# FFT-style convolution on one core: pixel loads of the next tile issued with the jobs that free their buffers, scratch loads and inverse jobs later, last planes sooner

## The chip, the cores and the metric

One core of a Trainium2 chip. The metric is device microseconds of one execution, the median over several runs. One execution of each kernel was also taken by the hardware profiler; the times within it are microseconds from the start of its span. Engines are called as the profile calls them: PE (TensorE matmuls), PEld (its weight loads), DVE (VectorE), ACT (ScalarE), POOL (GpSimd), SP (SyncE, which here only issues DMAs).

## The reference

A circular convolution of a 224x224 image of 96 channels with a 7x7 kernel, written through FFTs:

```python
wp = jnp.pad(w, ((0, H - K), (0, W - K), (0, 0), (0, 0)))
Xf = rfft2(x.astype(float32), axes=(1, 2))
Wf = rfft2(wp.astype(float32), axes=(0, 1))
Yf = jnp.einsum('bhwi,hwio->bhwo', Xf, Wf)
y = irfft2(Yf, s=(H, W), axes=(1, 2)).astype(bfloat16)     # x: 1x224x224x96, w: 7x7x96x96, bf16
```

## The kernel before

The kernel cuts the image into seven tiles of 32 columns. In each tile it transforms along the height with small matmuls (the forward jobs: pixels `xn` to spectra `xf`), convolves along the width for each of 17 spectral slots (the rounds, 33 matmuls each, on `xf` and on sums and differences `J` of it, the planes), writes the result to a scratch in DRAM (`scr`), loads it back in another layout (`tt`) and transforms back (the inverse jobs). Rounds of a tile are the frame; jobs of neighbouring tiles are slipped into each half round, so that PE stays full. DVE combines a round's products in two steps (`u` and `v`) and POOL adds them (the sum, `yf`), now and then DVE; POOL also copies the few columns that a tile shares with the tile before (the halo). Tiles 0 and 1 are convolved together in rounds r = 0 to 20, tile 1 four rounds behind; tile 2's forward jobs are part of that. Then tiles 2 to 6 follow one after another.

Each engine executes in program order, and SP issues nearly all DMAs: its order is the order in which the program text calls them. The four pixel buffers are reused by every tile.

```python
def pace(q, k):                 # q = [first half round, last, jobs, how many]
    a, b, jobs, n = q
    if k < a: return
    due = n if k >= b - 1 else -(-n * (k - a + 1) // (b - a))
    while jobs and n - len(jobs) < due:
        jobs.pop(0)()

def pump():                     # scratch loads, at most NTT = 5 tt buffers held
    while pend and held[0] < NTT:
        load_t(*pend.pop(0)); held[0] += 1
...
bursts = {}                     # (round, tile) -> which tile's planes are made there by DVE
for g in range(len(JGB)):       # groups of three slots, the last of two
    ...
    r1 = LAG + g0 - 1
    bursts[(r1, 0 if r1 < NS else 1)] = (1, g)
bursts[(NS + LAG - 1, 1)] = (2, 0)          # NS = 17, LAG = 4
for r in range(NS + LAG):
    for p in range(3):          # tile 2's forward jobs, in three parts
        if r == SH2[p + 1] + 1 - (p == 2):
            new_xf(2, SH2[p], SH2[p + 1])
            fj = f_jobs(2, p)   # p == 2: four jobs, two for each pair of pixel buffers
            if p == 2:
                fj += [lambda c=c: load_x(c) for c in range(12, 16)]     # tile 3's pixels
            add(2 * r, 2 * r + (8, 7, 4)[p], fj)
    if r == NS + 1:
        queue_c(0)              # tile 0's first scratch loads
    ...                         # the rounds of tiles 0 and 1
for t in range(2, NT):
    add(0, 26, a_jobs(t + 1))   # forward jobs of the next tile; starts with POOL's halo copy
    k1 = 2 * NS if t < TL else 2 * NS - 6
    km = 3 + -(-(k1 - 3) * nold // (nold + nnew))
    add(3, km, cj[:nold])       # inverse jobs
    ...
```

## Time and profile before

| | before |
|---|---|
| time, median (range) | 303.24 us (301.99 to 303.66, 4 runs) |
| PE busy, of a span of 300.3 us | 273.1 us, 91% |
| longest wait of PE in the program's middle | 8.16 us, for xn |
| half clock after it | 109.8 to 120.05 us |

A line of a timeline gives start, length, engine, operation, result and operands, their shape and how many instructions were merged; in brackets stands how long the engine had been idle and what ended that.

### The profile page before, as it was taken

The numbers are of one execution on the slowest core, as the hardware profiler recorded it, in microseconds if no ns is written. First come the engines' busy times: TensorE is split into PE (matmuls) and PEld (weight loads), VectorE is DVE, ScalarE is ACT, GpSimd is POOL, SyncE is SP. The second block draws the span as 40 slices with busy tenths as digits, with TensorE's granted clock in tenths as the row PEclk, the third lists the DMA queues.
The fourth block names the chain that finished last, engine by engine and source line by source line (L and its number), as shares of the span: only waits on it lengthen the run. The fifth ranks groups of instructions, "written<-read, shape, count | busy, mean of one in ns | idle before, by whom it ended". The sixth has DMA issues, their size and how long they took to land.

```text
span 300.3 us, 11988 instructions
## 1 busy us (share of the span) xinstructions
PE 273.1 (91%) x5010; PEld 246.0 (82%) x5010; DVE 227.9 (76%) x472; ACT 196.3 (65%) x488; POOL 112.3 (37%) x151
## 2 busy tenths in 40 slices
PE   8598998999999736999989999899999999999993
PEld 3488998989999726989889989798888989788872
DVE  7857399889797643686988879877897889967823
ACT  2456984766863412888578876788779875676313
POOL 6814022546536650234183235324264223243100
PEclk9955999999999985999999999999999999999998
DMA  7993340112111397577748686687727743776965
GB/s 179 170 219 98 83 123 35 41 43 81 44 41 43 106 201 219 143 188 197 219 105 224 195 224 195 187 218 211 232 89 185 224 138 102 197 197 174 251 127 183
DMA packets 45830, 46.04 MB, mean 153 GB/s; under 512 B 33626, under 2 KB 34758, under 8 KB 45678
## 3 DMA queue, kind: packets, MB, share of 16 engines
q1 hardware_dynamic: 43488, 43.21, 53.6%
q10 hardware_dynamic: 2288, 2.06, 2.4%
q8 instruction: 39, 0.64, 0.9%
q14 instruction: 15, 0.12, 0.1%
HBM read 23.92 MB, written 21.33 MB: 151 GB/s over the span
## 4 chain that ended last, share of the span: by engine, by line
PE 59%; DMA 13%; DVE 12%; issue 4%; ACT 4%; SPq 4%; POOL 1%; DVEq 0%; ACTq 0%; POOLq 0%
PE pb L86 59%; DVE J L86 5%; SPq L86 4%; DMA wq<-in_w_dram 3%; DVE v L86 2%; DMA xn<-in_x_dram 2%; DVE WF L86 2%; DMA xf<-scra 2%; ACT xf L86 2%; DVE u L86 2%; DMA scra<-yf 2%; DMA xf<-scrb 1%; DVE yf L86 1%; DMA scr<-yf 1%; ACT WF L86 1%
## 5 line engine op out<-in xcount | busy, mean ns | idle before, releaser
L86 PE MATMUL pb<-WF,J 96*128 96x96 bf16 x2898 | 169.9, 208 | 3.3 <-DVE J L86 2.2
L86 PEld LDWEIGHTS <-J 96*128 96x128 bf16 (+1 forms) x2910 | 144.2, 98 | 18.5 <-issue 9.9
L86 POOL TENSOR_TENSOR yf<-v,u 128x384 bf16<-128x384 f32 x85 | 83.9, 999 | 155.3 <-issue 103.6
L86 ACT CAST xf<-pb 96x408 bf16<-96x408 f32 (+3 forms) x150 | 68.3, 482 | 21.3 <-PE pb L86 18.8
L86 ACT CAST yo<-pb 84x384 bf16<-84x384 f32 (+1 forms) x144 | 61.3, 480 | 6.0 <-PE pb L86 4.5
L86 DVE TENSOR_TENSOR J<-xf 96x1824 bf16<-96x1824 bf16 (+1 forms) x84 | 63.2, 792 | 0.0
L86 PE MATMUL pb<-WF,xf 96*128 96x96 bf16 x952 | 61.0, 208 | 2.1 <-DVE WF L86 2.0
L86 PE MATMUL pb<-Fm,xn 118*128 118x136 bf16 (+3 forms) x576 | 52.4, 218 | 11.0 <-DMA xn<-in_x_dram 8.2
L86 PEld LDWEIGHTS <-xf 96*128 96x128 bf16 x952 | 47.8, 98 | 2.6 <-issue 1.5
L86 PEld LDWEIGHTS <-xn 118*128 118x128 bf16 x576 | 34.5, 101 | 12.5 <-DMA xn<-in_x_dram 8.3
L86 PE MATMUL pb<-tt,Gm 102*84 102x384 bf16 (+1 forms) x144 | 35.8, 329 | 0.6 <-DVE J L86 0.4
L86 ACT CAST WF<-pb 96x480 bf16<-96x480 f32 (+1 forms) x62 | 30.7, 570 | 5.1 <-PE pb L86 4.8
L86 PE MATMUL pb<-wq 98*128 98x120 bf16 (+1 forms) x336 | 26.3, 233 | 2.4 <-DMA wq<-in_w_dram 2.4
L86 DVE TENSOR_TENSOR J<-J 96x912 bf16<-96x912 bf16 (+1 forms) x42 | 27.6, 658 | 0.0
L86 PEld LDWEIGHTS <-wq 98*128 98x128 bf16 (+1 forms) x336 | 23.6, 151 | 3.9 <-POOL ct L86 2.6
L86 DVE TENSOR_TENSOR yf<-v,u 128x384 bf16<-128x384 f32 x27 | 15.4, 570 | 0.9
L86 POOL COPY xf<-xf 96x816 bf16<-96x816 bf16 (+3 forms) x16 | 15.7, 1010 | 0.0
L86 PEld LDWEIGHTS <-Gm 102*84 102x84 bf16 (+1 forms) x144 | 11.5, 114 | 3.0 <-DMA tt<-scr 0.6
L86 PE MATMUL pb<-wu 128*112 128x384 bf16 (+1 forms) x60 | 12.8, 376 | 1.1 <-DVE ct L86 1.1
L86 PEld LDWEIGHTS <-wu 128*112 128x112 bf16 (+1 forms) x60 | 7.3, 123 | 5.9 <-issue 1.9
L86 DVE TENSOR_TENSOR WF<-WF 96x960 bf16<-96x960 bf16 x15 | 11.1, 787 | 0.1
L86 DVE CAST xf<-pb 96x408 bf16<-96x408 f32 (+1 forms) x18 | 8.6, 516 | 1.9 <-PE pb L86 1.9
(388 smaller groups left out, 205.1 us busy)
## 6 DMA issues: line engine op xcount, KB each, us to landing
xn<-in_x_dram SPq DMA_DIRECT2D x28, 336.0 KB
scr<-yf SPq DMA_DIRECT2D x30, 288.0 KB
tt<-scr SPq DMA_DIRECT2D x24, 288.0 KB
out_dram<-yo SPq DMA_DIRECT2D x24, 252.0 KB
tt<-scr SPq DMA_DIRECT2D x12, 192.0 KB
out_dram<-yo SPq DMA_DIRECT2D x12, 168.0 KB
out_dram<-tt SPq DMA_DIRECT2D x4, 336.0 KB
scr<-yf SPq DMA_DIRECT2D x6, 192.0 KB
```

What stands on the lines that cost most here:

```text
L86: r = fn(*a, **k)
```

## The change

Its intent is to remove the hole in PE between the common stage of tiles 0 and 1 and tile 2. The whole of it is order:

```diff
-        r1 = LAG + g0 - 1
+        r1 = LAG + g0 - (3 if g == len(JGB) - 1 else 1)
         bursts[(r1, 0 if r1 < NS else 1)] = (1, g)
-    bursts[(NS + LAG - 1, 1)] = (2, 0)
+    bursts[(NS + LAG - 2, 1)] = (2, 0)
...
                 if p == 2:
-                    fj += [lambda c=c: load_x(c) for c in range(12, 16)]
-                add(2 * r, 2 * r + (8, 7, 4)[p], fj)
+                    for i in (1, 3):
+                        def fin(f=fj[i], i=i):
+                            f()
+                            for h in range(2):
+                                load_x(12 + 2 * h + i // 2)
+                        fj[i] = fin
+                add(2 * r, 2 * r + (8, 7, 5)[p], fj)
...
-        if r == NS + 1:
+        if r == NS + 3:
             queue_c(0)
...
-        km = 3 + -(-(k1 - 3) * nold // (nold + nnew))
-        add(3, km, cj[:nold])
+        k0 = 10 if t == 2 else 3
+        km = k0 + -(-(k1 - k0) * nold // (nold + nnew))
+        add(k0, km, cj[:nold])
```

## The prediction

> **What bounds the kernel now.** I read the page first, for the engine that is busiest and the place where it is not.
>
> ```profile
> span 300.3 us, 11988 instructions
> PE 273.1 (91%) x5010; PEld 246.0 (82%) x5010; DVE 227.9 (76%) x472; ACT 196.3 (65%) x488; POOL 112.3 (37%) x151
> ...
> PE   8598998999999736999989999899999999999993
> ...
> PEclk9955999999999985999999999999999999999998
> ```
>
> PE (the matmuls) is busy 91% of the span, so the time is PE's work plus PE's holes. In the slices of 7.5 us there is one hole away from the two ends: the digits 7, 3, 6 (98 to 120 us), and the granted clock falls to 8 and 5 in the last two. The program there ends the stage in which tiles 0 and 1 are convolved together and starts tile 2, which is exactly where the change works. Next I asked for the busy time in stretches cut at that hole (columns: PE, PEld, DVE, ACT, POOL busy, clock, DMA share, GB/s).
>
> ```profile
> 102.00:107.40 5.40, 3.55 (x80) 3.26 (x76) 3.33 (x9) 0.96 (x3) 1.83 (x2) 1.00 0.73 146
> 107.40:115.50 8.10, 0.00 (x0) 0.01 (x1) 2.30 (x4) 0.32 (x1) 2.77 (x4) 0.65 1.13 214
> 115.50:120.00 4.50, 4.48 (x53) 4.50 (x54) 2.72 (x5) 1.78 (x4) 0.00 (x0) 0.50 0.56 205
> 120.00:145.00 25.00, 25.00 (x497) 23.19 (x496) 18.38 (x40) 20.39 (x53) 7.89 (x8) 1.00 0.65 179
> ```
>
> For 8.1 us no matmul runs while DMA is full; then PE is busy again but at half clock until 120; from 120 PE has no idle time at all, and DVE (74%) and ACT (82%) have room. So a microsecond taken from this hole should shorten the kernel by one. The timeline of PE names what ends each hole:
>
> ```profile
> 104.04 0.34 PE L86 MATMUL pb<-WF,J 96*128 96x96 bf16 x4 [1.80 <-DVE J L86]
> ...
> 106.85 0.50 PE L86 MATMUL pb<-WF,xf 96*128 96x96 bf16 x8
> 115.52 0.50 PE L86 MATMUL pb<-Fm,xn 118*128 118x136 bf16 x3 [8.16 <-DMA xn<-in_x_dram]
> 115.81 1.33 PE L86 MATMUL pb<-WF,J 96*128 96x96 bf16 x14
> ...
> 119.13 1.20 PE L86 MATMUL pb<-WF,J 96*128 96x96 bf16 x14
> ```
>
> Two holes: 1.80 us for the last planes J of tile 1, and 8.16 us for the first pixels (xn) of tile 3, whose forward transform is interleaved with tile 2. Groups of 14 matmuls take 1.33 and 1.20 us after it; the same group takes 0.76 us from 121.6 us on. Why the pixels come so late is told by SP's queue, which issues all these loads in program order, and by the chain of work:
>
> ```profile
> 102.75 6.25 SPq L86 DMA_DIRECT2D tt<-scr  x10
> 109.11 5.38 SPq L86 DMA_DIRECT2D xn<-in_x_dram  x8
> 115.18 0.83 SPq L86 DMA_DIRECT2D scr<-yf  x2
> ```
>
> ```profile
> 99.39 3.31 DMA scr<-yf
> ...
> 106.92 2.09 SPq L86
> ...
> 109.49 5.89 DMA xn<-in_x_dram
> ```
>
> The pixels stand behind ten scratch loads (tt). Those cannot start before tile 0's last scratch write has landed (99.39 + 3.31 = 102.70), they then take until 109.0 to issue, and the pixel load takes 5.89 us behind their traffic. The buffers were free at about 100.8, when the last tile-2 forward matmuls ended. The path is thus: scratch write, tt issue, xn load, PE.
>
> **What the Trainium skill says.** "DMA: Bandwidth & Descriptors", section "Anatomy of one DMA", says that DMA engines do not wait on semaphores: any wait is on the issuing sequencer, before dispatch. The trace agrees: SP is silent from 99.71 to 102.75, and xn, which needed nothing from scratch, was held too. The same page, section "Specifications", puts the least transfer for line rate at 512 B. The tt packets here are 384 B: 226 GB/s at a DMA share of 1.02 (104 to 106 us), against 321 GB/s at 0.88 where mostly 3 KB pixel packets move (116 to 118), so it agrees in direction. "TensorE: Matmul & The Clock Gate", section "What's actually happening", says that an idle window of about 3.4 us halves the clock and a busy one restores it. Here the clock fell at 109.8, 2.5 us after the last matmul, and came back at 120.05, 4.5 us after the first: the windows are free-running, so only the size agrees. "GPSIMD Engine Reference", section "Specifications", says POOL shares its SBUF interfaces with VectorE. The trace agrees: the 96x912 plane sum takes 0.62 us alone (109.08) and 1.28 us while POOL copies the halo (153.90).
>
> **The change, part by part.** No arithmetic is added or removed: the built instruction streams have 10022 PE, 444 DVE, 67 POOL and 227 SP rows in both, and only two evacuations change to ACT (326 to 328 rows). Everything is order. (A round is one spectral slot's convolution, 33 matmuls; in each of its two halves waiting jobs of other stages are slipped in. xn 12 to 15 are tile 3's four pixel loads.)
>
> 1. Pixel loads. Each pair of tile 3's loads now follows the forward job that reads its two buffers last, and the tt loads are queued two rounds later. On SP the order becomes: last scratch write of tile 0, eight xn issues, the next scratch write, ten tt issues. I date this from the old trace. Forward job 1 ends on PE at about 99.8. SP must first pass tile 0's last write, which waits for POOL's sum. That sum was done at 99.37, but part 3 puts 1.39 us of planes (1.01 + 0.46, overlapped, at 102.97) in front of it: 100.75. Then xn 12 issues at about 101.2, xn 14 at 101.9, and 13 and 15 follow job 3 (PE, about 102.3). A pixel load with an idle DMA took 3.2 to 3.35 us from issue to its last semaphore step (the loads at 33 to 43 us), so xn 12 lands at 104.5 to 105, and the last of the four near 108.
> 2. When is xn 12 needed? PE reached that place at 107.35; without the J hole at 105.55. Margin 0.5 to 1 us, so the 8.16 us go. The second buffer (13) is needed six half rounds later, about 110: safe.
> 3. Planes. Tile 1's last planes move from round 18 to 16, ahead of use by three rounds: the 1.80 us go. Tile 2's first planes move one round up; in the old order they ran from 107.76 to 109.7 inside the xn hole, and would otherwise have become a new hole of over 1 us. In the new order their first operation ends near 105.2 and is needed near 105.6.
> 4. Clock. With no hole of several us, the half clock between 115.52 and 120.05 goes: half of 4.53 us, 2.27 us.
> 5. Inverse jobs of tile 2 start at half round 10 rather than 3: the same 12 jobs in 24 instead of 31 half rounds. This moves PE work, and it keeps PE from waiting for the tt loads, which now issue from about 104.8 and land by about 113; half round 10 is at 105.5 + 5 rounds of 1.75 us, about 114.
>
> Given back: about 0.3 us in round 18, because a PSUM bank waits for a DVE operation that now stands behind the moved planes (PE comes at 99.8, DVE frees it at 100.1); and about 1.1 us near tile 2's start. There DVE has a sum and three plane operations while POOL copies the halo, as at tile 3's start, where PE waited 1.09 us for DVE u (155.50) and at tile 4's about 1.0. In the old run this was masked: the halo copy ran at 110.7 inside the hole.
>
> Sum: 8.16 + 1.80 + 2.27 - 0.3 - 1.1 = 10.8 us. From the median of 303.2: 292.4 us.
>
> **Rivals.** (a) The pixels are still late. SP is one queue, and each issue also waits for the DMA eight before it; if the scratch write is released later, or the load is slowed by the 480 KB written just before it (those writes took 3.3 to 3.8 us against 2.07 alone), xn 12 lands 1 to 2 us late: 294 to 295. For: the margin is thin. Against: the DMA share is only 0.23 from 96 to 102.
> (b) DVE becomes the bound. Rounds 0 to 4 of tile 2 now lack inverse jobs: PE has 33 convolution matmuls (1.39 us) and two forward jobs (0.36), 1.75 us; DVE has about 1.7 us (u and v 0.81 at their spacing, a third of 2.0 us of planes and 0.57 of sum, about 0.86). Nearly equal, so 1 us more could be lost: 293.5.
> (c) The denser inverse jobs bind ACT or DMA. In rounds of two xf and two yo evacuations ACT is busy 82 to 84% and PE 100% (120 to 135 us), so ACT should hold. DMA was at 0.95 share from 130 to 135; my estimate for the new dense stretch is 220 GB/s, and five tt buffers give many us of slack. If it binds, 2 to 3 us: 295.
> (d) Nothing gained, because the hole moves to another wait. Against it: from 120 to 145 us PE is full, so no other chain is near.
>
> **Range and chances.** (a), (b) and (c) each cost 1 to 3 us and seldom all together; on the other side the 1.4 us given back may be absent: 290.5 to 296.0. Two per cent is 297.2, so faster needs only 6 of the 10.8 us: 0.95. Same 0.04, slower 0.01.
>
> **What would show it.** Right: no PE wait for xn, the J wait of 1.80 us gone, clock 1.00 from 31 us to the tail, xn issued near 101 before tt, a DVE wait of about 1 us within tile 2's first four rounds, none on tt. Wrong: a PE wait for xn of over 1 us near 105, a clock drop there, PE waits for tt after half round 10, or waits that make tile 2 much longer than 32 us from its first round to tile 3's (before: 106.85 to 149.33, less the 8.16 and 2.27).

## The result

The changed kernel takes 292.48 us (290.70 to 292.68, 4 runs) against 303.24: faster, ratio 0.9639 with a 95% interval of 0.9592 to 0.9686. It is the mean time of the one kernel's fast runs over that of the other's (292.08 over 303.03), so it is not quite the ratio of the two medians. In a second set of timing rounds (e9 below) it was 0.9647.

The page of the kernel after, the same four lines as before:

```profile
span 291.0 us, 11983 instructions
...
PE 272.5 (94%) x5010; PEld 244.2 (84%) x5010; DVE 229.6 (79%) x472; ACT 195.8 (67%) x488; POOL 113.1 (39%) x151
...
PE   8598998999999998999899998999999999999982
...
PEclk9955899999999999999999999999999999999997
```

PE's busy time is what it was (272.5 against 273.1 us); the digits 7, 3, 6 in its middle are gone and so is the dip of the clock. The stretches (PE, PEld, DVE, ACT, POOL busy, clock, DMA share, GB/s):

```profile
102.00:107.40 5.40, 5.40 (x131) 5.29 (x128) 4.30 (x10) 2.61 (x6) 3.12 (x5) 1.00 1.00 258
107.40:115.00 7.60, 6.55 (x141) 6.23 (x139) 7.13 (x12) 4.34 (x12) 5.77 (x6) 1.00 1.16 220
115.00:120.00 5.00, 4.73 (x97) 4.38 (x95) 4.53 (x11) 3.77 (x10) 1.96 (x2) 1.00 1.01 271
```

What was one empty stretch now holds 141 matmuls at full clock beside the same full DMA. About a microsecond of idle time is left in it, and DVE is busy 94% there (7.13 of 7.60). PE's timeline says where:

```profile
105.02 0.50 PE L86 MATMUL pb<-WF,xf 96*128 96x96 bf16 x8
105.41 0.34 PE L86 MATMUL pb<-Fm,xn 118*128 118x136 bf16 x3
...
110.55 0.34 PE L86 MATMUL pb<-WF,J 96*128 96x96 bf16 x4 [0.52 <-DVE J L86]
...
111.76 0.47 PE L86 MATMUL pb<-WF,J 96*128 96x96 bf16 x7 [0.53 <-DVE J L86]
```

The first matmuls on tile 3's pixels follow the last before them without a wait. Two holes of half a microsecond, for planes, are new. SP's queue shows the new order:

```profile
101.30 3.10 SPq L86 DMA_DIRECT2D xn<-in_x_dram  x8
105.07 0.34 SPq L86 DMA_DIRECT2D scr<-yf  x1
105.46 9.30 SPq L86 DMA_DIRECT2D tt<-scr  x10
```

And the chain of work no longer passes through a DMA or through SP in this stretch (start, length, what):

```profile
95.95 13.26 PE pb L86 x331
...
110.42 1.29 DVE J L86
...
111.76 4.02 PE pb L86 x85
```

Where did the time come from? The copy that ACT makes in the first round of a tile marks that tile's start: tile 2 at 107.44 before and 105.60 after (1.84 us sooner), tile 3 at 150.05 and 139.62 (10.43), tile 6 at 252.52 and 242.12 (10.40). So the gain is made before tile 3 and carried on unchanged (tile 0's start gives 0.12 us of it: 27.39 and 27.27). The two traced spans differ by only 9.3 us: the traced run of before was its fastest and that of after its slowest, and the traced tail differs (PE waits 1.13 us for a last scratch load, xf, in the run after). The medians differ by 10.8.

### The profile page after: what moved, and what is told of

Its sections match the earlier page's. It is cut to its first block, busy times and chain, and to the rows that moved or that the text cites. A ratio compares the mean times of both kernels' runs of the same rounds, so it can differ in the third digit from the quotient of the medians.

```text
span 291.0 us, 11983 instructions
## 1 busy us (share of the span) xinstructions
PE 272.5 (94%) x5010; PEld 244.2 (84%) x5010; DVE 229.6 (79%) x472; ACT 195.8 (67%) x488; POOL 113.1 (39%) x151
## 4 chain that ended last, share of the span: by engine, by line
PE 65%; DVE 14%; DMA 5%; issue 5%; POOL 4%; ACT 4%; SPq 1%; DVEq 0%; ACTq 0%; POOLq 0%
PE pb L86 65%; DVE J L86 6%; POOL ct L86 3%; DVE v L86 2%; DMA tt<-scr 2%; DVE u L86 2%; DMA xf<-scrb 2%; ACT xf L86 2%; DVE WF L86 1%; DVE yf L86 1%; DVE ct L86 1%; ACT WF L86 1%; POOL yf L86 1%; SPq L86 1%; DMA scrb<-yf 1%
## 5 line engine op out<-in xcount | busy, mean ns | idle before, releaser
L86 DVE TENSOR_TENSOR J<-xf 96x1824 bf16<-96x1824 bf16 (+1 forms) x84 | 64.4, 806 | 0.0
L86 DVE TENSOR_TENSOR J<-J 96x912 bf16<-96x912 bf16 (+1 forms) x42 | 28.3, 674 | 0.0
L86 POOL COPY xf<-xf 96x816 bf16<-96x816 bf16 (+3 forms) x16 | 16.7, 1073 | 0.0
L86 ACT CAST tt<-pb 112x384 bf16<-112x384 f32 x8 | 3.6, 479 | 9.7 <-PE pb L86 9.6
```

The costliest lines, as they stand in the source:

```text
L86: r = fn(*a, **k)
```

## The experiments

Ten runs, on the same chip in each group, each beside the kernel before. Times at the start (tile 0 began anywhere from 26.8 to 29.0 us) and at the tail vary by more than a microsecond from run to run, so besides the time I compare tile starts and PE's holes within the traces. A run that is over 1.5% above the fastest of its kernel counts as slow and is left out of the ratios; only e5 has such runs. A trace is one run, so differences of a few tenths between traces are less sure than the ratios.

### e1_loads_only: the pixel loads alone

The kernel before, with:

```diff
-                    fj += [lambda c=c: load_x(c) for c in range(12, 16)]
-                add(2 * r, 2 * r + (8, 7, 4)[p], fj)
+                    for i in (1, 3):
+                        def fin(f=fj[i], i=i): ...        # as in the change
+                        fj[i] = fin
+                add(2 * r, 2 * r + (8, 7, 5)[p], fj)
```

> Kernel before with the pixel-load part alone (planes, scratch-load round and inverse jobs as before). Theory (queue order: xn stood behind tt on SP): tile 0's last scratch write is passed at 99.4, xn 12 issues near 99.8 and lands near 103.3, so no xn wait of 8 us and no half clock; but the J hole of 1.8 us stays, tile 2's first planes become a new J hole of about 1 us near 107.5, and xn 13, still behind tt, lands near 115 and may cost 0.5 to 1 us. Sum about 8.16 + 2.27 - 1 - 0.5 - 1.1 = 7.8: 295.4 us (294.5 to 296.5). Rival (the loads were late because DMA was full of scratch traffic, not because of the queue): the xn wait stays above 4 us, time above 298.

Measured: 296.04 us (ratio 0.9795, 0.974 to 0.985), as the queue theory has it: less than before clear of noise, though the interval reaches across 2%. SP's queue, then PE's first matmuls on the two pairs of loads:

```profile
100.13 1.55 SPq L86 DMA_DIRECT2D xn<-in_x_dram  x4
101.78 7.92 SPq L86 DMA_DIRECT2D tt<-scr  x10
110.23 1.57 SPq L86 DMA_DIRECT2D xn<-in_x_dram  x4
```

```profile
106.41 0.34 PE L86 MATMUL pb<-Fm,xn 118*128 118x136 bf16 x3
...
115.57 0.34 PE L86 MATMUL pb<-Fm,xn 118*128 118x136 bf16 x3 [0.68 <-DMA xn<-in_x_dram]
```

The first load (xn 12) landed at 103.8, 3.7 us after its issue, with the ten tt issues right behind it; PE did not wait for it and the clock stayed full. PE's holes were 1.18 and 1.37 us for J, 0.77 for DVE u, and 0.68 for the pixels that stood behind tt. So most of the gain is a matter of who stands first in SP's queue. Full DMA engines are not the main cause, but they are part of it: from before to e1 the first pair of issues for xn 12 moved from 109.11 to 100.13 (8.98 us), and the time from there to its landing fell from 6.27 us (109.11 to 115.38) to 3.67, near the 3.35 to 3.62 us of such pairs at 33 to 43 us, where little else moves. The pair behind tt in e1 again took 5.2 us (110.23 to 115.44).

### e2_planes_only: the planes alone

The kernel before, with:

```diff
-        r1 = LAG + g0 - 1
+        r1 = LAG + g0 - (3 if g == len(JGB) - 1 else 1)
-    bursts[(NS + LAG - 1, 1)] = (2, 0)
+    bursts[(NS + LAG - 2, 1)] = (2, 0)
```

> Kernel before with the two plane moves alone. Theory (the end of this stretch is set by scratch write, tt issue, xn landing): the J hole of 1.80 us goes, but the xn hole grows by it, and because the moved planes delay POOL's sum and so tile 0's last scratch write by about 1.4 us, the whole chain slides: xn lands near 117, time 303.2 + 1.4 = 304.6 us (303.5 to 305.5), xn hole near 11 us. Rival (holes add, the plane part is worth its 1.80 us by itself): 301.4.

Measured: 302.86 us, ratio 1.0002 (0.9964 to 1.0041). Neither number was right, but the kind of answer was.

```profile
115.73 0.50 PE L86 MATMUL pb<-Fm,xn 118*128 118x136 bf16 x3 [9.90 <-DMA xn<-in_x_dram]
```

The J hole of 1.80 us vanished and the xn hole grew from 8.16 to 9.90 us by just as much. By itself this part is worth nothing. My slide of 1.4 us did not come: tile 0's last scratch write was indeed issued later, at 101.22 against 99.39 (1.5 us, after 0.4 us for a later start of tile 0 in this trace), but it landed in 1.87 us instead of 3.31, which fits that the write ahead of it (98.87, landed 101.97) was nearly through. It landed at 103.09 against 102.70, which is the same time after the same 0.4 us.

### e3_queue_early: the scratch loads early again

The changed kernel, with:

```diff
-        if r == NS + 3:
+        if r == NS + 1:
             queue_c(0)
```

> Kernel after, with the first scratch loads queued in round 18 again: xn 12 and 14 stay ahead of the ten tt issues, xn 13 and 15 fall behind them. Theory: no wait for the first pixels, but xn 13 issues near 110 and lands near 115, needed near 112: one xn wait of 2 to 4 us in tile 2's fourth round, perhaps no half clock; 295 us (294 to 297). Rival (only the first load matters, the delay of the scratch loads gains nothing): 292.5.

Measured: 299.39 us (ratio 0.988, 0.9827 to 0.9933), 2.4 us above the range.

```profile
112.22 0.47 PE L86 MATMUL pb<-WF,J 96*128 96x96 bf16 x7 [0.51 <-DVE J L86]
118.13 0.50 PE L86 MATMUL pb<-Fm,xn 118*128 118x136 bf16 x3 [5.44 <-DMA xn<-in_x_dram]
```

The second pair of pixel loads was issued only from 112.64, behind the ten tt issues, and PE waited 5.44 us for it. My miss had two parts: the issues ended later than I had dated them, and the hole was long enough for the clock, which was halved from 114.8 to 121.65. The kernel needs the whole pixel set ahead of the scratch loads, not only its first load. In e1 the same order cost little: PE came to that point some 3.8 us later (after the J holes and with inverse jobs in between), and SP issued them 0.8 us sooner, both counted from the start of tile 0.

### e4_inverse_early: the inverse jobs early again

The changed kernel, with:

```diff
-        k0 = 10 if t == 2 else 3
+        k0 = 3
```

> Kernel after, with tile 2's inverse jobs from half round 3 again. Theory: the first inverse job is due near 107.5, but the first tt landed at 113.3 in the changed kernel: PE waits for tt about 5 us, part of it in place of the 1.05 us J holes, and the clock may halve for some us: 297 us (295.5 to 299.5). Rival (tt loads have slack, the later start of the inverse jobs only evens out the load): within 1 us of 292.5.

Measured: 297.38 us (ratio 0.9814, 0.9759 to 0.987), within the range.

```profile
113.98 0.84 PE L86 MATMUL pb<-tt,Gm 102*84 102x384 bf16 x2 [3.79 <-DMA tt<-scr]
```

Tile 2 took 38.72 us instead of 34.02. The balance: a hole of 3.79 in place of 1.31 us, and half clock on 5.14 us (113.98 to 119.12), that is 2.48 + 2.57 = 5.05 against 4.70 measured. So the later start of the inverse jobs is no levelling of load; it pays for the scratch loads' new place in the queue.

### e5_xn_act: the loads on another queue

The kernel before, with tile 3's four loads issued from ACT instead of SP:

```diff
-                    fj += [lambda c=c: load_x(c) for c in range(12, 16)]
+                    fj += [lambda c=c: load_x(c, SE) for c in range(12, 16)]     # SE.dma_start, not SP's
```

> Kernel before with tile 3's first four pixel loads issued on ACT's DMA queue at the same place in the program, everything else as before: the tt loads still go out on SP from 102.75 and fill the same DMA engines. Theory (head of SP's queue): xn issues near 101 on ACT, lands near 105 (the first) to 110 (the last, beside tt); the 8.16 us hole shrinks to the J hole behind it, about 1 to 2 us, the half clock goes; ACT loses about 3 us to issuing, partly hidden: 296 us (294.5 to 298). Rival (DMA bandwidth): xn lands only when the tt traffic is over, after 111, and time stays above 300.

Measured: 302.44 us over four runs, of which two were slow (303.68 and 303.01); the two fast ones, 298.50 and 301.87, give a ratio of 0.993 (0.9823 to 1.0038). The traced run was a slow one, so I use it only for what waited for what, not for lengths to compare.

```profile
102.90 9.64 ACTq L86 DMA_DIRECT2D xn<-in_x_dram  x8
112.66 0.41 ACT L86 ACTIVATE tt__2662<-pb 128x288 f32<-128x288 f32 x1 [9.43 <-DMA tt<-scr]
```

The first load landed at 106.7, and PE did not wait for pixels; so far the queue theory holds. But a fall of the time to the 296 us expected did not show. In this program each DMA waits for the one issued eight places earlier, whichever queue it is on (here SP's tt at 111.36 and ACT's xn at 112.26 each start 0.02 us after that one landed), so ACT stood 9.43 us in its issues, its copies came late, DVE's planes after them, and PE had a hole of 4.56 us for J. I had put this at 3 us, partly hidden. In this trace the wait had only changed its engine. The clock was at half from 104.8 to 121.8, but that began in the J hole of 1.80 us that before has too, so it is not shown to come from the edit. As a test between the rivals e5 is weaker than e1, also because its first pair of issues (102.90) still went out before the first tt (103.54); as a warning it is worth having.

### e6_halo_late: POOL's halo copies later

The changed kernel, with the copies for tiles 3 to 6 kept back and issued after the sums of rounds 1 and 2:

```diff
+    late = []
...
-                apart(("A", t), ("halo", s0), GE.tensor_copy(out=o, in_=i))
+                if t > 2:
+                    late.append(lambda o=o, i=i: apart(("A", t), ("halo", s0), GE.tensor_copy(out=o, in_=i)))
+                else:
+                    apart(("A", t), ("halo", s0), GE.tensor_copy(out=o, in_=i))
...
+            def end(f=fills(qs, 2 * s + 1), s=s):
+                f()
+                if s in (1, 2) and late:
+                    late.pop(0)()
...                                                # b_round then calls end
```

> Kernel after, with POOL's two halo copies for tiles 3 to 6 moved from a tile's start to behind the sums of its rounds 1 and 2. Theory (the holes at a tile's start come from the planes running at half speed beside those copies): the plane operations of tile 2's round 0 take 1.4 + 0.6 us instead of 2.9 + 1.3, the 1.05 us of J holes at 110 to 112 go, as do 0.8 and 0.95 us at the starts of tiles 3 and 4: 289.7 us (288.8 to 291). Rival (DVE is simply overfull at a tile's start, with two sets of planes and two sums): holes of the same size remain, 292.5.

Measured: 289.89 us (ratio 0.9605, 0.9541 to 0.967), as expected; but the interval overlaps the changed kernel's, so it is e10 below that shows the gain by time. DVE's planes of tile 2's round 0, in the changed kernel:

```profile
107.58 2.92 DVE L86 TENSOR_TENSOR J<-xf 96x1824 bf16<-96x1824 bf16 x2
...
110.42 1.28 DVE L86 TENSOR_TENSOR J<-J 96x912 bf16<-96x912 bf16 x1
```

and in e6:

```profile
107.66 2.25 DVE L86 TENSOR_TENSOR J<-xf 96x1824 bf16<-96x1824 bf16 x2
...
109.83 0.62 DVE L86 TENSOR_TENSOR J<-J 96x912 bf16<-96x912 bf16 x1
```

The second operation halves; the first is still slower than the 1.40 us of the same planes at 104.52 in the changed kernel, when POOL is idle: POOL's sums run from 106.67 to 108.6 beside it. PE's idle time fell from 0.91 to 0.07 us in tile 3 and from 0.95 to 0 in tile 4, and those tiles became 1.1 and 1.3 us shorter. In tile 2 it did not fall: the copies now slowed a sum and the planes of round 3, and one hole came back.

```profile
117.34 0.33 PE L86 MATMUL pb<-WF,J 96*128 96x96 bf16 x4 [1.68 <-DVE u L86]
```

### e7_warm_hole: the clock term by itself

The kernel before, with 44 matmuls of zeros into an unread bank as the first job of tile 2; the result stays correct.

```diff
+    def warm():
+        pwu = bank()
+        for _ in range(44):
+            TE.matmul(pwu[:, 0:384]..., lhsT=wu[:], rhs=wu[:]..., start=True, stop=True)
...
+        if t == 2:
+            add(0, 1, [warm])
         if t + 1 < NT:
             add(0, 26, a_jobs(t + 1))
```

> Kernel before with 44 matmuls of zeros (128x384, about 7.2 us) put on PE inside the 8.16 us hole, into a bank that nobody reads; nothing else changed. It measures the clock term by itself. Theory (half of 4.53 us is lost to the clock): no half clock before the tail, first xn matmul still near 115.5, time 303.2 - 2.3 = 300.9 us (300.2 to 301.6). Rival (the matmuls after the hole are limited by something else than the clock, DVE for example): 303.2.

Measured: 301.32 us, but with runs from 298.51 to 302.92 the ratio (0.9958, 0.9875 to 1.0041) decides nothing. The trace does:

```profile
106.70 7.32 PE L86 MATMUL pb<-wu 128*128 128x384 bf16 x44
114.32 0.34 PE L86 MATMUL pb<-Fm,xn 118*128 118x136 bf16 x3 [0.30 <-DMA xn<-in_x_dram]
```

With the hole filled the clock stayed full. From the first matmul on tile 3's pixels to the start of tile 3 it took 32.42 us (114.32 to 146.74), against 34.53 before (115.52 to 150.05): the half clock costs 2.11 us, where the prediction had 2.27.

### e8_no_planes: the change without the planes

The changed kernel, with:

```diff
-        r1 = LAG + g0 - (3 if g == len(JGB) - 1 else 1)
+        r1 = LAG + g0 - 1
-    bursts[(NS + LAG - 2, 1)] = (2, 0)
+    bursts[(NS + LAG - 1, 1)] = (2, 0)
```

> Kernel after, with both plane moves undone. Theory: the J hole of 1.8 us is back and tile 2's first planes make another of about 1 us; tile 0's last scratch write is 1.4 us earlier, which gains nothing, because xn is in time either way: 295.1 us (294.2 to 296). Rival (planes are off the path once the loads are in time): 292.5.

Measured: 293.72 us (ratio 0.9724, 0.9657 to 0.979). PE's holes:

```profile
103.26 0.34 PE L86 MATMUL pb<-WF,J 96*128 96x96 bf16 x4 [1.18 <-DVE J L86]
...
108.13 0.77 PE L86 MATMUL pb<-WF,J 96*128 96x96 bf16 x14 [1.37 <-DVE J L86]
```

Tile 3 starts 1.43 us later than in the changed kernel (141.05 against 139.62; tile 0's start differs by 0.17). The plane moves, worthless alone, are worth about 1.3 us once the loads are in time, by these two traces; the ratios' intervals overlap (0.9657 to 0.979 here). I had expected 2.6: the first hole is 1.18 and not 1.80, because tile 2's last forward jobs, now spread into round 18, fill part of it (e1 spreads them too and also has 1.18), and the 1.37 stands in place of the 1.05 at 110 to 112, not beside it.

### e9_after_again and e10_halo_late2: the changed kernel again, and the halo copies later still in tile 2

e9 is the changed kernel again. e10 is e6 with one line different:

```diff
-                if s in (1, 2) and late:
+                if s in ((7, 8) if t == 2 else (1, 2)) and late:
```

> The changed kernel itself, unaltered, timed in the same rounds as the next run so that a 3 us difference can be read: 292.5 us (291.5 to 293), ratio to before 0.965, holes of 0.52 and 0.53 us for J in tile 2's third round as in its first trace.

> As e6_halo_late, but in tile 2 alone the two halo copies stand behind the sums of rounds 7 and 8 instead of 1 and 2, where they slowed the next planes and left one hole of 1.68 us (DVE u). Theory (DVE is behind in tile 2's first rounds, because two sets of planes were made within two rounds, and has caught up by round 7): that hole falls to at most 0.5 us, tiles 3 to 5 keep theirs near zero: 3.3 us under the changed kernel of the same rounds, 289.2 us (288.3 to 290). Rival (any place of the copies costs DVE the same): the hole reappears near round 9, 290.2.

Measured in the same timing rounds: e9 291.88 us (ratio to before 0.9647, 0.9616 to 0.9678), e10 288.82 us (0.9546, 0.9516 to 0.9575): 3.1 us less than the changed kernel and 14 less than before. What is left of the hole in tile 2:

```profile
116.38 0.33 PE L86 MATMUL pb<-WF,J 96*128 96x96 bf16 x4 [0.27 <-DVE u L86]
```

Tile 2 takes 32.64 us instead of e9's 34.03. No hole came back near round 9, so the theory that DVE is behind in tile 2's first rounds and has caught up by round 7 stands. Whether e10 beats e6 is not shown: they ran in different rounds, and their intervals overlap.

## Why the prediction was right

The time (292.4 predicted, 292.48 measured) agrees better than its terms deserve: some errors cancelled. All the signs named for "right" were seen: no wait for xn or tt in tile 2, the J wait of 1.80 us gone, full clock from 31.7 us to the tail, xn issued at 101.30, and DVE waits of 1.3 us in tile 2.

- **Pixel loads, 8.16 us.** Right in cause and size, and shown by e1. The steps held to a few tenths: the scratch write passed at 100.89 (predicted 100.75), xn issued from 101.30 (101.2), the first load complete at 105.27 (104.5 to 105). It was needed at 105.41. The margin was thus 0.1 us, not 0.5 to 1, and rival (a) was closer to coming true than its weight in the range said. The last of the four landed at 110.5, not near 108; this did no harm, since the second buffer in use (xn 13) landed at 109.15 and was read at 112.07.
- **Planes, 1.80 us.** The hole went, and tile 2 started 1.84 us sooner. But the sum added it as if it were free-standing. e2 and e8 show that it is worth 0 without the loads and about 1.3 us with them.
- **Clock, 2.27 us.** Right; e7 measures 2.11.
- **Inverse jobs.** Counted as protection only, with tt landing by about 113. It landed from 113.3 (the first) to 118.7 (the fifth): SP needed 9.30 us for the ten issues, not the 6.25 of before, since they had to wait for the xn loads eight places ahead (the second tt issue starts at 107.67, and that load landed at 107.65). The first inverse matmul came at 115.72, 2.4 us after its load. e4 shows the size of what was avoided, 4.7 us within tile 2.
- **0.3 us given back in round 18.** Wrong. PE is busy without a break from 96 to 107.4 us. It began round 18 at 100.01, before the DVE operation that I had made it wait for ended (99.71 + 0.34 = 100.05); the matmul at 100.01 waits for a semaphore of ACT instead. I had the wrong engine.
- **1.1 us given back at tile 2's start.** Right in size (0.52 + 0.53, and 0.27 at 117.19 us) and in cause (POOL's halo copies beside DVE's planes, by e6 and e10), though the profile puts it down to J where I had said u.

By tile starts the sum reads: 1.84 + 8.08 + 2.11 come to 12.03 (0.08 us of the hole of 8.16 lies before tile 2's mark); tile 3 gained 10.43; so 1.60 went back within tile 2, of which 1.31 is idle time seen in the trace. The other 0.3 us is PE time that counts as busy: tile 2 less its idle time takes 32.71 us in the changed kernel, but 32.41 in e6 and 32.37 in e10, so it went when the halo copies were moved; how it arises stays open. Rivals (b) and (c) did not come true: after 112 us PE's holes in tile 2 are 0.27 us in all.

Two readings in the prediction are wrong, though nothing rests on them. From 116 to 118 us the pixels' 3 KB packets are 0.26 of 0.64 MB; the rest are packets of 1.5 and 2.25 KB, so the rates compare 384 B packets with larger ones, not with pixel packets alone. And the traces do not show two evacuations changing to ACT: ACT has 488 instructions in both, DVE 472.

## What to carry to other kernels

When one engine issues all loads, look at what stands before a late load in that queue and whether it needs it: here pixels that depended on nothing waited behind scratch loads that depended on a write just issued. A repair of the order moves the wait to whatever was put back (the scratch loads), so move that one's consumer too, and count each part with the others in place: parts that are worth nothing alone can be worth most of their hole once the longer one is gone. Moving a load to a computing engine's queue can move the wait into that engine, as in e5's trace.

## What the Trainium skill lacked or had wrong

- "TensorE: Matmul & The Clock Gate", section "Why this matters for your kernels", advises against PE gaps of over about 3 us, because one idle window halves the clock. Here shorter ones were enough: 2.43 us at the start of before (12.29 to 14.72; half clock from 14.24), 2.13 in e7 (12.29 to 14.42), 1.80 in e5 (a slow run). The clock changes of ten traces (before, after, e1 to e8) lie on a grid of 3.41 us, and a grid window that was idle in part was enough. Between 31 and 270 us the clock was halved after a window with 1.45, 2.11, 2.46, 2.64 or 3.41 us of idle PE (e5, e4, before, e3, e2) and kept after windows with up to 1.44 us (e6 had 1.44, e7 1.38, e8 1.37). The 1.80 us hole of before was cut by the grid into 0.75 and 1.05 and did no harm. But this is no rule for idle time alone: near the ends of e7 it was halved after 1.00 us (13.42 to 16.84) and kept after 1.77 (289.90 to 293.32). Full clock came back only after a window without any idle time seen, but not after every such window (before: none from 17.65 to 24.48, and half clock until 31.31).
- "GPSIMD Engine Reference", section "Specifications", names the contention with VectorE without a size. Here both sides pay: DVE's plane operations took 2.92 + 1.28 us instead of 1.40 + 0.62, and POOL's two copies 2.71 instead of 1.67 us (the first plane operations also ran beside POOL's sums, and spans on POOL are rough).
